# Removing sixteen small diagnostic loads, and the waits on them, from the end of a decode-attention kernel

## The chip, the cores and the metric

The kernel runs on one core of one Trainium2 chip. The metric is the device time of that core in microseconds. Two words: a transfer has landed when the last of the DMA engines that carry it has raised its semaphore, and a ring is the list of transfers that wait on one DMA engine for one queue.

## The reference, cut to what matters

Two attention blocks for a single query token. Block A has 32 heads with 32768 keys each. Block B has 32 query heads on 8 key/value heads and looks at the last 4096 keys only. Each is followed by a projection with `wo` (4096 x 512), and the two results are put side by side.

```python
def _A_ref(x, k_cache, v_cache, wq, wo):
    q = transpose((x @ wq).reshape(B, Sq, H, Dh), 0, 2, 1, 3)
    scores = einsum("bhqd,bhkd->bhqk", q, k_cache) * (Dh ** -0.5)
    o = einsum("bhqk,bhkd->bhqd", softmax(scores), v_cache)
    return transpose(o, 0, 2, 1, 3).reshape(B, Sq, H * Dh) @ wo
# _B_ref: the same with k and v cut to the last 4096 keys and repeated 4 times
return concatenate([a, b], axis=-1)          # (1, 1, 1024)
```

The caches of A alone are 2 x 32 x 8 MiB. Every byte is read once and used for one query, so this is a kernel of loads.

## The kernel before

SyncE issues nearly all loads on one queue, in program order, with its own waits for free buffers ahead of them. The part that the change touches stands at the end of the plan:

```python
for g in range(NQH):                     # 32 heads of A
    self.load_k(g, ...); self.load_v(g)  # 8 MiB each
    ...                                  # transposes, scores, softmax, P x V
self.loop = {}
for n in ("B", "A"):                     # the projections' weights, 4 MiB each
    for part in range(len(self.WO_CUTS[n]) - 1):
        self.load_wo(n, part)            # B in 2 pieces, A in 5
for i in range(16):                      # the sixteen diagnostic loads, "marks"
    self.load(self.marks[0:i + 1, 16 * i:16 * i + 16], self.X["A"]["wo"][0:i + 1, 0:16], self.marksem[i])
self.emit_spread("A")
self.emit_proj()                         # projections, store of B's half, store of A's half
for i in range(16):
    self.op("sp", lambda e, i=i: e.wait_ge(self.marksem[i], 16))
for n in ("B", "A"):
    self.op("sp", lambda e, n=n: e.wait_ge(self.outsem[n], 16))
```

Load `i` brings `i + 1` rows of 32 B into a buffer that nobody reads. B's half of the result is stored as one row (issued near 1313 us), A's half as two rows of 512 B from partitions 0 and 64; that is the last store:

```python
self.op("sp", lambda e: e.dma_start(self.out[0, :, off:off + 512].rearrange("a (i x) -> (a i) x", i=2),
                                    self.out_sb[0:65:64, :]).then_inc(self.outsem[name], 16), o)
```

Of the kernel before, what the change touches and what calls it, by code (L numbers as in the profile page):

```python
# [3 lines left out]
BF16 = mybir.dt.bfloat16  # L4
# [49 lines left out]
class _Kernel:  # L54
# [118 lines left out]
    def emit(self, eng):  # L173
# [22 lines left out]
        def body(e):  # L196
# [17 lines left out]
            for k, it in enumerate(need):  # L214
                cur, plan = {}, []
                for n in it:
                    w = []
                    for name, (sem, val) in n.items():
                        if name not in sems:
                            continue  # L220
                        rel = val - start[name] - step[name] * k
                        if rel > cur.get(name, 0):
                            cur[name] = rel
                            w.append((name, rel))
                    plan.append(sorted(w))
                plans.append(plan)
            for k, plan in enumerate(plans):
                for p, q in zip(plan, plans[-1]):
                    assert p == q or (k == 0 and set(p) <= set(q)), (eng, k, p, q)
# [37 lines left out]
    def alloc(self):  # L267
        nc = self.nc
        sb = nc.alloc_sbuf_tensor
        self.kbuf = sb("kbuf", [128, 3 * HALF * DH], BF16, align_bytes=4096)  # L270
        self.vbuf = sb("vbuf", [128, 2 * HALF * DH], BF16, align_bytes=4096)
        self.kt = [sb(f"kt{i}", [128, 1024], BF16) for i in range(NKT)]
        self.psb = sb("psb", [128, 512], BF16)
        self.ptsb = sb("ptsb", [128, 512], BF16)
        self.ident = sb("ident", [128, 128], BF16)
        self.ones = sb("ones", [128, 128], BF16)
        self.e32 = sb("e32", [128, 32], F32)
        self.spread = sb("spread", [32, 4 * 129], BF16)
        self.tr = {k: sb(f"tr_{k}", [128, 32], F32) for k in ("in", "a")}
        self.rows64 = sb("rows64", [128, 64], F32)  # L280
        self.nscale = sb("nscale", [1, 128], F32)
        self.m4 = sb("m4", [1, 128], F32)
        self.pb = sb("pb", [128, 512], F32)
        self.out_sb = sb("out_sb", [128, 256], BF16)
        self.marks = sb("marks", [16, 17 * 16], BF16)
        self.c = {}
        for name, d in self.X.items():
            HG = d["HG"]
            self.c[name] = dict(
                x=sb(f"x_{name}", [128, 12], BF16),  # L290
                oc=[sb(f"oc_{name}{i}", [128, DH + 1], F32) for i in range(2 if name == "B" else 1)],
                b=sb(f"b_{name}", [128, 32], F32),
                cm=sb(f"cm_{name}", [128, 32], F32),
                mr=sb(f"mr_{name}", [1, HG], F32),
                nb=sb(f"nb_{name}", [128, 2], F32),
                hot=sb(f"hot_{name}", [128, d["nb"]], F32),
                lh=sb(f"lh_{name}", [128, HG], F32),
                hsel=sb(f"hsel_{name}", [128, 64], F32),
                rinv=sb(f"rinv_{name}", [32, 1], F32),
                ob=sb(f"ob_{name}", [32, DH], BF16),  # L300
                oz=sb(f"oz_{name}", [128, 32], BF16),
            )

        self.qz = sb("qz", [128, 32 * self.X["B"]["NKVH"] + 64], BF16)
        self.qa = sb("qa", [128, NQH], BF16)
        self.qrow = sb("qrow", [128, 512], BF16)
        self.qw = sb("qw", [128, 64], BF16)
        self.hw = sb("hw", [128, 32], F32)
        ps = nc.alloc_psum_tensor
        self.S = ps("psS", [128, 512], F32)  # L310
        self.T = [ps(f"psT{i}", [128, 512], F32) for i in range(NT)]
        self.PT = ps("psPT", [128, 512], F32)
        self.ACC = ps("psACC", [128, 512], F32)
        self.G = ps("psG", [128, 512], F32)
        s = nc.alloc_semaphore
        self.ksem = [s(f"ksem{i}") for i in range(2)]
        self.vsem = [s(f"vsem{i}") for i in range(2)]
        self.xsem = {n: s(f"xsem_{n}") for n in self.X}
        self.wosem = {n: [s(f"wosem_{n}{i}") for i in range(len(self.WO_CUTS[n]) - 1)] for n in self.X}
        self.outsem = {n: s(f"outsem_{n}") for n in self.X}  # L320
        self.marksem = [s(f"marksem{i}") for i in range(16)]



# [69 lines left out]
    def plan(self):  # L394
        self.lsem = {"k": self.ksem, "v": self.vsem}
        self.fill = {w: [0, 0] for w in "kv"}
        self.free = {"k": [None] * 3, "v": [None] * 2}
        self.nbatch = 0
        self.copies = []
        self.pending = []  # L400
        self.psread = self.ptread = self.sread = self.accread = None
        self.gath = self.qcopy = self.hcopy = self.qread = None
        self.constants()
        a, b = self.X["A"], self.X["B"]

        self.load_wq("B")
        self.load_b("k", 0)
        self.load_wq("A")
        self.load_b("k", 1)
        self.emit_qproj("B")  # L410
        self.emit_unit("B", 0)
        self.emit_qproj("A")
        self.emit_stats("B", 0)
        self.emit_unit("B", 1, {1: lambda: self.emit_PT("B", 0)})
        self.emit_stats("B", 1)
        for g in range(2):
            if g == 1:
                self.emit_PT("B", g)
            self.load_b("v", g)
            self.emit_PV("B", g)  # L420
        self.emit_spread("B")

        for g in range(NQH):
            self.loop = {"pe": g, "dve": g // 2}
            self.load_k(g, 1 if 0 < g < NQH - 1 else 2)
            self.load_v(g)
            self.emit_qcopy(g)
            self.emit_unit("A", g)
            self.emit_stats("A", g)
            self.emit_PT("A", g)  # L430
            self.emit_PV("A", g)
        self.loop = {}
        for n in ("B", "A"):
            for part in range(len(self.WO_CUTS[n]) - 1):
                self.load_wo(n, part)
        for i in range(16):
            self.load(self.marks[0:i + 1, 16 * i:16 * i + 16], self.X["A"]["wo"][0:i + 1, 0:16], self.marksem[i])
        self.emit_spread("A")
        self.emit_proj()
        for i in range(16):  # L440
            self.op("sp", lambda e, i=i: e.wait_ge(self.marksem[i], 16))
        for n in ("B", "A"):
            self.op("sp", lambda e, n=n: e.wait_ge(self.outsem[n], 16))

# [335 lines left out]
```

## Time and profile before

| | before |
|---|---|
| time, median of 6 runs | 1324.16 us |
| span of the profiled run | 1322.0 us |
| bytes, mean rate | 570.6 MB, 432 GB/s |
| last piece of A_wo landed | 1318.87 us |
| last store issued / landed | 1319.90 / 1321.49 us |
| the sixteen loads: issued, landed | 1286.99 to 1308.00, last at 1320.64 us |

From the page of the kernel before, the DMA share in 40 slices (9 is 90% or more), the rate in the same slices, and the packet counts in all and of SyncE's queue:

```profile
DMA  9999999999999999999999999999999999999998
GB/s 404 434 435 435 436 432 436 434 436 434 431 436 436 428 438 434 430 438 432 434 436 432 434 434 434 436 432 434 437 430 436 436 430 436 434 432 436 432 434 359
DMA packets 13489, 570.60 MB, mean 432 GB/s; under 512 B 1827, under 2 KB 1830, under 8 KB 2214
...
q1 hardware_dynamic: 13190, 570.44, 99.8%
```

The engines that move the data are full until the last slice, which holds the end. A kernel like this ends when its bytes are in, plus whatever has to follow the last of them. The chain that ended last, in order of time (start, duration, what), shows how short that is:

```profile
1286.51 32.36 DMA kbuf<-in_A_wo_dram
1318.87 0.04 issue
1318.92 0.51 PE psPT L724 x6
1319.43 0.02 issue
1319.45 0.42 DVE out_sb L729
```

The last piece of A_wo is issued at 1286.51 and lands 32.36 us later, since all that was queued before it has to move first; six matmuls and one cast follow. The timeline of SyncE's issues in the same stretch (start, duration, what):

```profile
1284.72 2.23 SPq L326 DMA_DIRECT2D kbuf<-in_A_wo_dram  x5
1286.99 21.01 SPq L326 DMA_DIRECT2D marks<-in_A_wo_dram  x16
1313.40 0.24 SPq L744 DMA_DIRECT2D out_dram<-qrow  x1
1319.90 0.59 SPq L730 DMA_DIRECT2D out_dram<-out_sb  x1
```

The sixteen small loads keep SyncE for 21.01 us. SPq and ACTq are the instruction queues of SyncE and ScalarE. SyncE's waits (for whom: us in all, times, longest) show how much of it could be on the critical path:

```profile
SPq L730 <- DVE out_sb L729: 6.2, 1, 6.2
SPq L744 <- DVE qrow L743: 5.4, 1, 5.4
SPq L443 <- DMA out_dram<-out_sb: 0.5, 1, 0.5
```

After the small loads SyncE waits another 5.4 us for B's row and 6.2 us for A's.

### The profile page before, as it was taken

The page shows a single profiled execution, that of the slowest core. Times are in us where ns is not written, and L with a number is a line of the kernel's source. Part 1 is how long each engine was busy: PE and PEld are TensorE (multiplying, and loading weights), DVE is VectorE, ACT ScalarE, POOL GpSimd, SP SyncE. Part 2 cuts the span into 40 slices and gives each one's busy share as a digit, 9 for nine tenths or more (in the row PEclk, how much of TensorE's full clock was granted, in tenths as well). Part 3 has the DMA queues.
Part 4 walks back from the last instruction along what each step waited for, and adds up shares of the span by engine and source line. Part 5 has one row for each costly group of instructions (what it writes and reads, how often), then busy time and mean ns, then how long its engine had stood idle before and what let it go on. Part 6 is the DMA issues. An engine that isn't in the chain of part 4 may idle for free. (4 is left out here: it accounts for less than half of the span.)

```text
span 1322.0 us, 28805 instructions
## 1 busy us (share of the span) xinstructions
PE 966.2 (73%) x13243; PEld 674.9 (51%) x13243; DVE 751.3 (57%) x1341; ACT 54.8 (4%) x167; POOL 2.6 (0%) x22
## 2 busy tenths in 40 slices
PE   4675668777767877677787876778787677868686
PEld 3453446555444655444465544446554444655453
DVE  3663456665545666554566655556655555666463
ACT  0000000000000000000000000000000000000000
POOL 0000000000000000000000000000000000000000
PEclk8887798888779887877988788798878878888798
DMA  9999999999999999999999999999999999999998
GB/s 404 434 435 435 436 432 436 434 436 434 431 436 436 428 438 434 430 438 432 434 436 432 434 434 434 436 432 434 437 430 436 436 430 436 434 432 436 432 434 359
DMA packets 13489, 570.60 MB, mean 432 GB/s; under 512 B 1827, under 2 KB 1830, under 8 KB 2214
## 3 DMA queue, kind: packets, MB, share of 16 engines
q1 hardware_dynamic: 13190, 570.44, 99.8%
q8 instruction: 8, 0.13, 0.0%
q10 hardware_dynamic: 288, 0.00, 0.0%
q14 instruction: 3, 0.02, 0.0%
HBM read 570.43 MB, written 0.00 MB: 432 GB/s over the span
## 5 line engine op out<-in xcount | busy, mean ns | idle before, releaser
L563 DVE COPY kt<-psT 128x1024 bf16<-128x1024 bf16 x1056 | 654.9, 684 | 237.5 <-PE psT L559 235.7
L559 PE MATMUL psT<-ident,kbuf 128*128 128x128 bf16 x8448 | 579.1, 234 | 168.5 <-DMA kbuf<-in_A_k_cache_dram 154.6
L559 PEld LDWEIGHTS psT<-ident,kbuf 128*128 128x128 bf16 x8448 | 539.3, 106 | 261.0 <-DMA kbuf<-in_A_k_cache_dram 162.7
L662 PE MATMUL psACC<-vbuf,ptsb 128*4 128x512 bf16 (+1 forms) x2112 | 185.2, 527 | 23.2 <-ACT ptsb L637 21.3
L582 PE MATMUL psS<-kt,qw 128*32 128x512 bf16 x2048 | 157.6, 384 | 15.3 <-DVE kt L563 15.3
L676 DVE TENSOR_SCALAR oc_A<-psACC,hot_A 128x128 f32<-128x128 f32 x32 | 11.2, 351 | 250.1 <-PE psG L689 250.1
L662 PEld LDWEIGHTS psACC<-vbuf,ptsb 128*4 128x4 bf16 (+1 forms) x2112 | 60.4, 110 | 138.2 <-issue 91.0
L610 ACT ACTIVATE psb<-psS,nb_A 128x512 bf16<-128x512 f32 x32 | 22.0, 687 | 1165.4 <-DVE nb_A L609 1165.4
L582 PEld LDWEIGHTS psS<-kt,qw 128*32 128x32 bf16 x2048 | 34.0, 95 | 57.9 <-DVE kt L563 31.3
L689 PE MATMUL psG<-oc_A,hw 128*32 128x128 f32 (+1 forms) x128 | 19.3, 227 | 52.3 <-DVE oc_A L678 52.3
L689 PEld LDWEIGHTS psG<-oc_A,hw 128*32 128x32 f32 x128 | 11.4, 109 | 62.4 <-DVE oc_A L678 55.1
L634 PE MATMUL psPT<-ident,psb 128*128 128x128 bf16 x136 | 18.0, 275 | 34.0 <-ACT psb L610 34.0
L678 DVE SCALAR_TENSOR_TENSOR oc_A<-psACC,hot_A,oc_A 128x128 f32<-128x128 f32 x96 | 33.7, 351 | 3.4
L599 DVE TENSOR_REDUCE tr_in<-psS 128x1 f32<-128x512 f32 x34 | 23.5, 692 | 17.1 <-PE psS L582 17.1
L634 PEld LDWEIGHTS psPT<-ident,psb 128*128 128x128 bf16 x136 | 10.2, 117 | 37.0 <-ACT psb L610 36.7
L603 PE MATMUL psACC<-rows,tr_in 128*1 128x64 f32 x64 | 8.7, 217 | 25.5 <-DVE tr_in L599 25.5
L637 ACT ACTIVATE ptsb<-psPT 128x512 bf16<-128x512 bf16 x34 | 20.3, 597 | 31.1 <-PE psPT L634 31.1
L603 PEld LDWEIGHTS psACC<-rows,tr_in 128*1 128x1 f32 x64 | 2.7, 80 | 35.1 <-DVE tr_in L599 35.1
L607 PE MATMUL psACC<-mr_A,nscale 1*128 1x1 f32 x64 | 12.1, 256 | 9.7 <-DVE mr_A L606 9.7
L607 PEld LDWEIGHTS psACC<-mr_A,nscale 1*128 1x128 f32 x64 | 9.4, 182 | 15.7 <-DVE mr_A L606 15.7
L609 DVE COPY nb_A<-psACC 128x1 f32<-128x1 f32 x32 | 5.0, 157 | 15.0 <-PE psACC L607 15.0
L501 PE MATMUL psACC<-vbuf,x_B 128*2 128x512 bf16 x32 | 3.6, 627 | 13.5 <-DMA x_B<-in_B_x_dram 13.5
(81 smaller groups left out, 75.7 us busy)
## 6 DMA issues: line engine op xcount, KB each, us to landing
kbuf<-in_A_k_cache_dram SPq DMA_DIRECT2D x4, 4096.0 KB, 22.2
kbuf<-in_B_k_cache_dram SPq DMA_DIRECT2D x2, 4096.0 KB, 31.7
vbuf<-in_B_v_cache_dram SPq DMA_DIRECT2D x2, 4096.0 KB, 24.7
vbuf<-in_B_wq_dram SPq DMA_DIRECT2D x1, 4096.0 KB, 12.5
vbuf<-in_A_wq_dram SPq DMA_DIRECT2D x1, 4096.0 KB, 32.2
kbuf<-in_B_wo_dram SPq DMA_DIRECT2D x2, 2048.0 KB, 33.3
kbuf<-in_A_wo_dram SPq DMA_DIRECT2D x1, 1408.0 KB, 27.7
kbuf<-in_A_wo_dram SPq DMA_DIRECT2D x1, 1024.0 KB, 29.7
```

The lines of the kernel that those rows point to most:

```text
L559: inst = e.transpose(T[:, 128 * k:128 * k + 128], src[:, DH * k:DH * k + DH], self.ident[:, :])
L563: self.copies.append(self.op("dve", lambda v: v.tensor_copy(KT[:, :], T[:, :]), o, to="pe"))
L582: inst = e.matmul(self.S[32 * c:32 * c + 32, :], lhsT=win, rhs=self.kt[(bb + c // 2) % NKT][:, 512 * (c % 2):512 * (c % 2) + 512], start=b ...
L599: o = dve(lambda v: v.reduce_max(tr["in"][:, 0:1], self.S[:, :], axis=AXX), self.sdone, self.k_pool, to="pe" if name == "A" else None)
L603: o = self.op("pe", lambda e: e.matmul(self.ACC[0:1, 0:64], lhsT=tr["in"][:, 0:1], rhs=self.rows64[:, :], start=True, stop=True, skip_grou ...
L607: o = self.op("pe", lambda e: e.matmul(self.ACC[:, 64:65], lhsT=self.nscale[:, :], rhs=t["mr"][0:1, :], start=True, stop=True, skip_group_ ...
L610: self.sread = self.op("act", lambda s: s.activation(out=self.psb[:, :], in_=self.S[:, :], func=ACTF.Exp, bias=t["nb"][:, k:k + 1], scale= ...
L634: inst = e.transpose(PT[:, 128 * jj:128 * jj + 128], self.psb[:, 128 * jj:128 * jj + 128], self.ident[:, :])
L637: self.ptread = self.op("act", lambda s: s.activation(out=self.ptsb[:, :], in_=PT[:, 0:512], func=ACTF.Copy), self.psread, to="pe")
L662: inst = e.matmul(acc[32 * c:32 * c + rows, 0:512], lhsT=lhsT, rhs=rhs, start=begin, stop=end, tile_position=(0, 32 * c), skip_group_check ...
L678: o = self.op("dve", lambda v, src=src, hot=hot: v.scalar_tensor_tensor(out=oc, in0=src, scalar=hot, in1=oc, op0=ALU.mult, op1=ALU.add), p ...
L689: return self.op("pe", lambda e: e.matmul(self.G[0:32, c0 + c:c0 + c2], lhsT=win, rhs=t["oc"][g % len(t["oc"])][:, c:c2], start=False, sto ...
```

## The change

The loads are for diagnosis: load `i` runs on `i + 1` of the sixteen DMA engines, and from its completion one can see when those engines come to the end of the queue. The intent of the change is to take the instrument out. The diff, whole but for file names:

```diff
-        self.marks = sb("marks", [16, 17 * 16], BF16)
...
-        self.marksem = [s(f"marksem{i}") for i in range(16)]
...
             for part in range(len(self.WO_CUTS[n]) - 1):
                 self.load_wo(n, part)
-        for i in range(16):
-            self.load(self.marks[0:i + 1, 16 * i:16 * i + 16], self.X["A"]["wo"][0:i + 1, 0:16], self.marksem[i])
         self.emit_spread("A")
         self.emit_proj()
-        for i in range(16):
-            self.op("sp", lambda e, i=i: e.wait_ge(self.marksem[i], 16))
         for n in ("B", "A"):
             self.op("sp", lambda e, n=n: e.wait_ge(self.outsem[n], 16))
```

## The prediction

> What bounds the kernel. Its loads. The page gives 570.6 MB at a mean of 432 GB/s over a span of 1322.0 us, with a DMA share of 9 tenths or more in all slices but the last. In the steady part each pair of 4 MiB loads lands about 38.63 us after the pair before, 434 GB/s; the median K load lands 27.6 us after its issue (DMA issues) though it needs only 9.7 us of the engines, so the queue never runs dry. PE (73%) and DVE (57%) have slack; SyncE's 1243 us of waits for PE only pace the queue.
>
> The end (chain of waits, timeline). The last piece of A_wo is issued at 1286.5 us and lands at 1318.87, because loads are queued ahead. Then come six projection matmuls (0.51 us), the cast to out_sb (0.42), the issue of the last store (0.59, from 1319.90), its landing at about 1321.5, and about 0.45 us of closing synchronisation. The other store is issued at 1313.40.
>
> What is removed. Sixteen loads of 1 to 16 rows of 32 B, 136 data packets of 9 ns, and their completion increments. SyncE issues them from 1286.99 to 1308.00 (21.01 us, 0.256 to 7.59 us each). That looks large, but SyncE has nothing else to do until 1313.40, so it is hidden; most of it looks like back-pressure.
>
> Do they delay the real loads? The Trainium skill (DMA: Bandwidth & Descriptors, "Queues, rings and completion order") says that each DMA engine consumes descriptors in ring order. The marks come behind all of wo. The trace agrees: their packets start only from 1316.6, and on the slowest engine, which ends wo at 1318.87, its marks land after that (to about 1320.6). wo lands over the engines with a spread of 2.0 us, as K and V do without marks. The 8 MiB of wo come at 428 GB/s against 434, but its packets are smaller (121 ns for 3 KB, 2418 ns for 64 KB: about 9 ns each beyond what their bytes need), which explains that. I expect nothing here, at most 0.1 us.
>
> Do they delay the end? (a) The marks drain on the first engines until about 1320.3; the last store, on two engines, is issued at 1319.90-1320.49, and its packets start at 1321.12. It is hardly blocked, but its issue took 592 ns where the other store took 243, perhaps because the marks' completions are still being handled: 0 to 0.35 us. (b) The sixteen waits run from 1320.55 to 1321.02, while the store is under way (landed about 1321.49). They cost nothing, but for one that seems to stand behind the last store's wait: about 0.065 us. The other store, behind the marks on one engine, lands at 1320.5; nobody waits for it.
>
> Other effects: later small buffers move by 544 B in SBUF; nothing measurable expected.
>
> Prediction: 1324.14 minus about 0.25, so 1323.9 us; 8 in 10 between 1323.2 and 1324.4. Faster by over 2%: 0.01; within 2%: 0.98; slower: 0.01.
>
> What would show it: the marks and SyncE's 21 us vanish from the timeline; the last A_wo piece still lands at 1318.8 to 1318.9; the last store's issue takes 0.25 to 0.6 us and it lands up to 0.4 us sooner.
>
> What would make it wrong: the marks slow the wo loads after all (wo lands before 1318.7); the blocked SyncE, or marks in the rings, hold back something I don't see; or the new addresses change PE or DVE enough to let the queue run dry.

## The result

| | before | after |
|---|---|---|
| time, median of 6 runs | 1324.16 us (1323.98 to 1324.72) | 1324.18 us (1324.08 to 1324.66) |
| span of the profiled run | 1322.0 us | 1322.1 us |
| last piece of A_wo landed | 1318.87 us | 1318.96 us |
| last store: issue to landing | 1319.90 to 1321.49, 1.59 us | 1319.99 to 1321.59, 1.60 us |
| landing to end of span | 0.47 us | 0.46 us |
| B's store landed | 1320.53 us | 1317.05 us |

The ratio is 1.0 (95% interval 0.9987 to 1.0013). So the times show no difference, though one below 1.7 us could hide in the interval; that the change is worth nothing is read from the traces. Here and below a ratio compares all fast runs, so it is not quite the ratio of the medians that I quote.

The same lines of the page of the kernel after:

```profile
DMA packets 13217, 570.59 MB, mean 432 GB/s; under 512 B 1555, under 2 KB 1558, under 8 KB 1942
...
q1 hardware_dynamic: 12918, 570.43, 99.7%
```

SyncE's queue has 272 packets less (13190 - 12918): 136 rows of 32 B, and 136 increments of a semaphore, one for each load and engine. The chain that ended last:

```profile
1286.50 32.47 DMA kbuf<-in_A_wo_dram
1318.96 0.04 issue
1319.01 0.51 PE psPT L718 x6
1319.52 0.02 issue
1319.54 0.42 DVE out_sb L723
```

Piece by piece it is the chain of before, 0.09 us later. That tenth was there ahead of the changed code: the last V load landed at 1299.29 us before and at 1299.40 after. SyncE's issues and its waits:

```profile
1284.69 2.24 SPq L324 DMA_DIRECT2D kbuf<-in_A_wo_dram  x5
1313.34 0.32 SPq L738 DMA_DIRECT2D out_dram<-qrow  x1
1319.99 0.59 SPq L724 DMA_DIRECT2D out_dram<-out_sb  x1
```

```profile
SPq L738 <- DVE qrow L737: 26.4, 1, 26.4
SPq L724 <- DVE out_sb L723: 6.3, 1, 6.3
SPq L437 <- DMA out_dram<-out_sb: 1.0, 1, 1.0
```

The 21.01 us of issue went straight into SyncE's wait for B's row: 5.4 + 21.0 = 26.4 us. The sixteen waits behind the last store went into the wait for that store's landing, which shows as 1.0 us where it was 0.5. And the last store's issue takes 0.59 us in both kernels.

So the useful questions are why the small loads cost nothing, how near they were to costing something, and where the 0.25 us that I had forecast went.

### The profile page after: what moved, and what is told of

Same layout as the page of the kernel before. It is cut to its first block, busy times and chain, and to the rows that moved or that the text cites. A ratio compares the mean times of both kernels' runs of the same rounds, so it can differ in the third digit from the quotient of the medians.

```text
span 1322.1 us, 28781 instructions
## 1 busy us (share of the span) xinstructions
PE 967.8 (73%) x13243; PEld 677.1 (51%) x13243; DVE 752.5 (57%) x1341; ACT 54.8 (4%) x167; POOL 2.6 (0%) x22
## 3 DMA queue, kind: packets, MB, share of 16 engines
q1 hardware_dynamic: 12918, 570.43, 99.7%
## 5 line engine op out<-in xcount | busy, mean ns | idle before, releaser
L683 PE MATMUL psG<-oc_A,hw 128*32 128x128 f32 (+1 forms) x128 | 19.3, 227 | 52.4 <-DVE oc_A L672 52.4
```

The source lines that it names most:

```text
L683: return self.op("pe", lambda e: e.matmul(self.G[0:32, c0 + c:c0 + c2], lhsT=win, rhs=t["oc"][g % len(t["oc"])][:, c:c2], start=False, sto ...
```

## The experiments

My theory: the small loads were free because of their place. They stand behind every real load on the same rings, SyncE had idle time, and their landings ended before the last store's. The rivals: (R1) they did cost a few tenths, and something in the kernel after costs the same again; (R2) they are free because they are tiny, wherever they stand. All medians of "before" below are from the same chip. The outputs are right.

### e1: the buffer and the semaphores alone

```diff
 # against the kernel before
-        for i in range(16):
-            self.load(self.marks[...], ..., self.marksem[i])
...
-        for i in range(16):
-            self.op("sp", lambda e, i=i: e.wait_ge(self.marksem[i], 16))
```

> The buffer and the sixteen semaphores stay, the loads and the waits go: it tells a shift of the later buffers by 544 B from the loads. Theory (the marks are free, nothing compensates them): time within 0.3 us of before and after, last A_wo piece lands at 1318.8 to 1319.0, last store's issue to landing 1.6 us. Rival (the loads cost some tenths, and the new addresses in the kernel without marks cost the same again): 0.2 us or more below before, with an earlier landing of A_wo or a shorter end.

Measured: 1324.27 us against 1324.27 for before (ratio 0.9997, interval 0.998 to 1.0014), A_wo at 1318.92 us, the last store from issue to landing 1.59 us. R1's shifted addresses are not seen. But this profiled run took 1324.65 us, and its span of 1322.6 us was 0.5 above the others. Its chain shows why (start, duration, what):

```profile
1309.67 3.27 PE psS L733 x32
1312.94 0.02 issue
1312.96 0.70 DVE pb L736
1313.67 0.04 issue
1313.71 1.02 PE psACC L737 x2
1314.73 2.27 PE psT L741 x11
1317.00 3.04 PE psPT L720 x43
```

Here TensorE, not A_wo, ended last. B's projection ran from 1309.60 to 1312.91, 3.3 us where the kernels before and after took 1.90. Two stretches of the same profile, then of the kernel after (stretch, length, busy times of TensorE, its weight loads, VectorE, ScalarE and GpSimd, granted TensorE clock, DMA share, GB/s):

```profile
1305.00:1310.00 5.00, 2.56 (x40) 0.98 (x33) 2.09 (x7) 0.00 (x0) 0.00 (x0) 0.84 1.00 426
1310.00:1315.00 5.00, 4.20 (x37) 1.15 (x30) 0.93 (x2) 0.00 (x0) 0.00 (x0) 0.75 0.99 417
```

```profile
1305.00:1310.00 5.00, 2.56 (x48) 1.21 (x44) 2.09 (x7) 0.00 (x0) 0.00 (x0) 1.00 0.98 420
1310.00:1315.00 5.00, 4.20 (x31) 1.10 (x25) 1.37 (x2) 0.00 (x0) 0.00 (x0) 1.00 0.99 419
```

The clock granted in the last 20 us differs from run to run (0.84 and 0.75 against 1.00 and 1.00), and where it is low here and in e9 (0.84 and 0.71), the projections finish after the last load. This is a source of scatter of about half a microsecond that does not hang on the change: it is seen without the loads here and with them in e9. That it also made the slowest runs of before (1325.54 us) is likely but not shown; those runs have no profile.

### e2 and e3: the waits moved

A kernel with the loads and without any wait on them was not run, since it would end with loads that nobody waits for; that variant stays open. Instead e2 moves the waits to ScalarE, which is idle by then, and e3 puts them ahead of the last store on SyncE.

```diff
 # e2, against the kernel before
-            self.op("sp", lambda e, i=i: e.wait_ge(self.marksem[i], 16))
+            self.op("act", lambda e, i=i: e.wait_ge(self.marksem[i], 16))
```

> The sixteen loads stay; the waits go from SyncE to ScalarE, which is idle then. Theory: the waits were hidden under the last store's landing, so the end of the span after the store's landing stays at 0.47 us (before) or loses at most 0.07 us, and the span stays within 0.2 us of 1322.0. Rival (the waits cost their 0.47 us): span 0.4 us shorter.

Measured, one look: 1324.06 us, span 1322.0 us, and 0.46 us from the last store's landing to the end. The theory holds: the waits were hidden, wholly. What I had taken for one wait too many behind the last store (0.065 us in the prediction) is not there either.

```diff
 # e3, against the kernel before
+        for i in range(16):                       # now just ahead of the last store
+            self.op("sp", lambda e, i=i: e.wait_ge(self.marksem[i], 16))
         self.store("A", self.PT, 0, o)
...
-        for i in range(16):
-            self.op("sp", lambda e, i=i: e.wait_ge(self.marksem[i], 16))
```

> The same loads and waits, but the waits stand ahead of the last store on SyncE. Theory: the marks' last landing is at 1320.64, the store is otherwise issued at 1319.90, so the store is issued at 1320.7 to 1321.1 and the kernel gets 0.8 to 1.2 us longer. Rival (marks and waits are free because they are tiny, wherever they stand): no change over 0.2 us.

Measured: 1325.07 us (1324.91 to 1325.11) against 1324.27 (1323.97 to 1325.54), 0.8 us more by the medians. The ratio's interval (0.9987 to 1.002) contains 1, because two runs of before were slow; but no run of e3 was under 1324.9, and five of the seven of before were. The timeline of SyncE has the last store where it was forecast:

```profile
1320.76 0.60 SPq L728 DMA_DIRECT2D out_dram<-out_sb  x1
```

The last of the small loads landed at 1320.61 us. But in this profile TensorE was late too: the cast ran from 1320.15 to 1320.57, so that without the waits the store would have been issued at about 1320.60, 0.03 us after the cast as in before. Of the delay in this profile the waits made only the last 0.15 us. The other three runs, all a little longer, have no profile. What the trace does show is a floor: with the waits there the store can't be issued before the last small load has landed, at 1320.61, against 1319.90 in before. That is an estimate of 0.7 us for a run in which TensorE is in time. The times fit it and speak against R2, but e3 alone doesn't settle it; e4, e6 and e10 do.

### e4: the small loads ahead of wo

```diff
 # against the kernel before
+        for i in range(16):
+            self.load(self.marks[...], ..., self.marksem[i])
         for n in ("B", "A"):
             for part in range(len(self.WO_CUTS[n]) - 1):
                 self.load_wo(n, part)
-        for i in range(16):
-            self.load(self.marks[...], ..., self.marksem[i])
```

> The sixteen loads go onto SyncE's queue ahead of all loads of wo. Theory A (order in the rings protected the real loads, and a mark holds its ring for the 0.17 to 0.2 us that lay between its landings in the trace of before): the slowest engine, with nine marks, and the first ones, with up to sixteen, lose 1.5 to 3.2 us; A_wo's last piece lands at 1320 to 1322, time 1325.3 to 1327. Theory B (a mark costs its ring only its packets, 2 x 9 ns each, so at most 0.3 us): time within 0.4 us of before, A_wo lands by 1319.3. Rival C (SyncE's 21 us of issue are a cost that was hidden): loads of wo issued some 20 us later, a gap in the queue, several us longer.

Measured: 1325.03 us (1324.99 to 1325.10) against 1324.16 (1323.93 to 1325.22): 0.87 us more by the medians, with A_wo at 1319.78. The ratio's interval contains 1 here too (0.9989 to 1.0022); six of the seven runs of before lie below all four of e4. Neither A (1320 to 1322) nor B (by 1319.3) is right: the truth lies between. SyncE's issues:

```profile
1273.15 5.73 SPq L326 DMA_DIRECT2D marks<-in_A_wo_dram  x16
1278.93 0.88 SPq L326 DMA_DIRECT2D kbuf<-in_B_wo_dram  x2
1284.79 11.62 SPq L326 DMA_DIRECT2D kbuf<-in_A_wo_dram  x5
```

Rival C falls, and the 21 us are explained: the sixteen loads now take 5.73 us to issue, and it is the five pieces of A_wo that take 11.62 us where they took 2.23. The length belongs to whoever issues next when the rings are full, not to the small load.

What a small load costs its ring can be worked out from the semaphore records of the trace: from the mean landing over the sixteen engines of the last V load to that of A_wo it is 19.58 us before and 20.41 us here. The sixteen loads put 8.5 of them on an engine on average (136 / 16), so each holds its ring for (20.41 - 19.58) / 8.5, about 0.10 us. That is less than the 0.17 to 0.20 us between their landings, and some five times the 18 ns of its two packets.

### e5: the small loads on ScalarE's queue

```diff
 # against the kernel before
-            self.load(self.marks[...], ..., self.marksem[i])
+            self.op("act", lambda e, i=i: e.dma_start(
+                self.marks[...], ...).then_inc(self.marksem[i], 16))
```

> The sixteen loads go to ScalarE's queue, whose rings are empty, issued after the last head's work at about 1300 us, in the midst of wo's loads. Theory A (a mark holds up its engine for 0.2 us wherever it runs): A_wo lands 1 to 3 us later. Theory B (only packets of 9 ns, and another ring's data goes on meanwhile): A_wo lands within 0.3 us of 1318.9, time within 0.4 us. Both: SyncE's 21 us disappear from its timeline; ScalarE's issue takes under 8 us in all if SyncE's long issues were back-pressure from full rings, some 21 us if they are the price of such a load itself.

Measured: 1324.05 us (1323.86 to 1324.27) against 1324.16, A_wo at 1318.65 us. ScalarE's issues after the last head's work:

```profile
1299.46 0.49 ACTq L437 DMA_DIRECT2D marks<-in_A_wo_dram  x1
...
1299.98 5.47 ACTq L437 DMA_DIRECT2D marks<-in_A_wo_dram  x15
```

Some 6 us of issue, as the back-pressure account has it, and theory B for the rings. The packets of the small loads moved from 1303.2 to 1314.0, in the midst of wo, on the same DMA engines. The mean from V to A_wo is 19.67 us, so a small load cost (19.67 - 19.58) / 8.5, about 0.01 us: its packets, and no more. (In the ten other kernels, which have no small loads ahead of wo, this mean lies between 19.57 and 19.58 us, so 0.09 us stands clear of the noise.) The contrast with e4 is instructive. The same 136 rows on the same engines cost ten times as much on the ring that carries the real loads. The Trainium skill (DMA: Bandwidth & Descriptors, "Issuing engines are not separate DMA queues") says that issuing from several engines saves only the sequencer's time, because all run on the same sixteen DMA engines. For large loads this has nothing to set against it. For these small ones, about 0.09 us each was saved besides. But e5 changed two things: the queue, and the spacing, since the packets came over 10.8 us among large ones where in e4 they came within 2.1 us, one behind another. Which of the two saved the time was not tested. That an engine fills the pauses of one ring with packets of another is my reading of it; no run shows the inside of an engine.

### e6: thirty-two loads

```diff
 # against the kernel before
-        for i in range(16):
-            self.load(self.marks[...], ..., self.marksem[i])
+        for r in range(2):
+            for i in range(16):
+                self.load(self.marks[... 272 * r + 16 * i ...], ..., self.marksem[i])
...
-            ... e.wait_ge(self.marksem[i], 16))
+            ... e.wait_ge(self.marksem[i], 32))
```

> Thirty-two loads instead of sixteen, at the same place, ended by waits for both. Theory (free only while they drain before the last store needs the rings and SyncE): the second sixteen land on the first two engines one every 0.17 to 0.2 us after the first, until about 1323.2, so the last store's data starts some 1.5 to 2.8 us later and the kernel gets 1.5 to 3 us longer; the store of B's half is issued later than 1313.4. Rival (the loads are too small to matter): within 0.3 us of before.

Measured: 1325.92 us (1325.83 to 1326.04) against 1324.16 (1323.93 to 1325.22), 1.76 us more, with all four runs above all seven. (Ratio 1.0012, interval 0.9995 to 1.0028.) The size was right, and B's store was issued later, at 1314.93, as expected; the way was not. The last store was issued as ever, and its data packets started at 1321.02 us, not later:

```profile
1319.80 0.59 SPq L732 DMA_DIRECT2D out_dram<-out_sb  x1
```

Only its landing was late:

| us | before | e6 |
|---|---|---|
| start of the last data packet of a small load | 1318.6 | 1318.5 |
| start of the first data packet of the last store | 1321.13 | 1321.02 |
| B's store landed | 1320.53 | 1323.25 |
| last store landed, the later of its two engines | 1321.49 | 1323.43 |

So a small load's cost here is in its completion. On one engine the increments come one after another, 0.17 to 0.2 us apart, long after the data, and a later transfer's increment stands behind them.

### e8, e9, e10: more loads of one row

This account says that what counts is the number of small loads on the last store's engines, not the sum over all engines. A load of one row runs on the first engine alone, so sixteen of them give that engine as many more as e6 did, with 16 instead of 136 completions.

```diff
 # against the kernel before; n = 4, 8, 16
         for i in range(16):
             self.load(self.marks[...], ..., self.marksem[i])
+        for j in range(n):
+            self.load(self.marks[0:1, ...], self.X["A"]["wo"][0:1, 0:16], self.marksem[0])
...                    # marks grows by 16 * n columns; marksem[0] is waited for at 16 * (n + 1)
```

> Four more loads of one row after the sixteen; all go to the first engine. Theory (landings of one engine come 0.177 us apart, in order, and the last store's landing waits for those ahead of it on its engines; before had 1321.49 - 1320.53 - 0.18, about 0.8 us, to spare): B's store lands at about 1321.2, the last store is not delayed, time within 0.2 us of before. Rival (the sum of small loads over all engines counts, as the doubling's 136 rows cost 1.8 us): 4 rows cost 0.05 us. Here both say no change.

> Eight more loads of one row. Theory: B's store lands at about 1321.95, the last store at about 1322.1, so +0.4 to +0.8 us in time; its data packets are read at 1321.1 as ever. Rival (sum over all engines): +0.1 us.

> Sixteen more loads of one row, 16 completions more where the doubling had 136. Theory (one engine's row of landings): B's store lands at about 1323.3, the last store at about 1323.5, +1.6 to +2.1 us, as much as the doubling. Rival (sum over all engines): +0.2 us.

| extra one-row loads | time, median (lowest to highest), us | B's store landed | last store landed, its two engines |
|---|---|---|---|
| none (before, same chip) | 1324.20 (1323.82 to 1325.09) | - | - |
| 4 | 1324.39 (1323.93 to 1324.73) | 1320.72 | 1321.62, 1321.63 |
| 8 | 1324.48 (1324.35 to 1325.04) | 1322.00 | 1322.47, 1322.48 |
| 16 | 1326.04 (1325.74 to 1326.09) | 1323.30 | 1321.79, 1323.48 |

The ratios are 1.0, 1.0 and 1.0012; none of their intervals excludes 1, so again what separates e10 is that all its runs lie above all of before, and the trace. With sixteen the cost is 1.84 us, as much as for the doubling with its 136, and the rival falls. The last line shows it best: one row of the last store landed at 1321.79, 1.59 us after the issue as in before, and the other, on the engine with the extra loads, 1.69 us later, though both were issued by one instruction:

```profile
1320.20 0.59 SPq L732 DMA_DIRECT2D out_dram<-out_sb  x1
```

SyncE's waits in e10 name the row of B, which stands ahead of it on that engine:

```profile
SPq L445 <- DMA out_dram<-qrow: 2.0, 1, 2.0
```

With four loads nothing is visible in the time, as both sides expected. But B's store landed at 1320.72, not at the 1321.2 forecast: the first engine landed its first small load at 1317.09, 0.53 us earlier than in before (1317.62). The order in which the engines finish differs from run to run, and the room that is left differs with it. With eight the time is 0.28 us up by the medians, under the 0.4 to 0.8 that I expected, and the profile can't decide: TensorE was late in it as in e1, so the store was issued at 1320.89 and landed 1.59 us later, undelayed, although B's store landed at 1322.00 as forecast. So the threshold is not pinned down. It lies between 4 and 16 loads and depends on how late the store is anyway.

The Trainium skill (DMA: Bandwidth & Descriptors, "Queues, rings and completion order") says that each engine's increment is a strongly ordered write that lands only after that engine's earlier writes. The landings here agree: e10's 1321.79 and 1323.48 differ by engine, and on the slower one the last store lands after B's, as they were issued. The page's rule for the number of engines ("Why a DMA increments its semaphore by 16 and not by 1": the largest number up to 16 that divides the row counts of both sides) agrees too: a load of `i + 1` rows shows `i + 1` landings for every `i` from 0 to 15.

### e7: the last store in two

My prediction read the 592 ns of the last store's issue as a delay by the small loads. The kernel after has the same 592 ns, so that is false. What is it, then?

```diff
 # against the kernel after
-        self.op("sp", lambda e: e.dma_start(<both rows>, self.out_sb[0:65:64, :]).then_inc(...), o)
+        for i, q in enumerate(("sp", "act")):
+            self.op(q, lambda e, i=i: e.dma_start(<row i>, self.out_sb[64 * i:64 * i + 1, :]).then_inc(...), o)
+        self.op("dve", lambda v: v.tensor_copy(self.m4[0:1, 0:1], self.m4[0:1, 1:2]))   # carries the second signal
...                                                            # A's outsem is waited for at 32
```

> The kernel without marks, with the last store of two 512 B rows split in two stores of one row, one issued by SyncE and one by ScalarE (a small copy on VectorE between them carries the second signal). If the 592 ns of the last store's issue come from its two rows on two engines, each one-row store is issued in 0.24 to 0.33 us, as B's was, and the end from out_sb to the close gets 0.1 to 0.3 us shorter. If 592 ns are the price of a store at that moment, each takes 0.55 us or more and nothing is gained.

The end of the timeline (start, duration, engine, what):

```profile
1319.58 0.42 DVE L723 CAST out_sb<-psPT 65x256 bf16<-65x256 f32 x1 [3.69 <-PE psPT L718]
1319.92 0.13 DVE L727 COPY m<-m 1x1 f32<-1x1 f32 x1
1320.04 0.51 ACTq L725 DMA_DIRECT2D out_dram<-out_sb  x1
1320.08 0.25 SPq L725 DMA_DIRECT2D out_dram<-out_sb  x1
```

SyncE's one-row store is issued in 0.25 us, at the same moment of the kernel, so the 592 ns belong to the form of the two-row store and not to the moment. Two rows alone don't explain them: the small load of two rows was issued in 236 ns in e4 and in 249 ns in e5. What in that store takes the time (its direction, its rows 64 partitions apart) stays open. ScalarE's store takes 0.51; the first of its loads in e5 took 0.49 and the fifteen after it 0.25 to 0.41, so in both kernels the first issue on that queue after compute was a long one. Both landed by 1321.33, 1.33 us after the cast's end at 1320.00; in the kernel after this took 1.62 us (1319.96 to 1321.59). The gain of 0.30 us is real in the trace and lost in the times: 1324.15 us (1323.84 to 1324.80) against 1324.16 for before. It is the one version that should beat both kernels, by 0.02%.

## Why the prediction was right or wrong

The forecast of 1323.9 us with "within 2%" at 0.98 held: 1324.18 us lies in the range of 1323.2 to 1324.4. The range was wide enough to hold no gain at all, so the number says little for the 0.25 us, which did not come. Point by point:

- "The queue never runs dry", and the time is the bytes plus a short end: right. The rate is 432 GB/s in both, and the chain of after is that of before. One figure in it is off: the loads of the steady part are 8 MiB each, not 4 (two of them in 38.63 us are the 434 GB/s), so a K load needs 19.3 us of the engines, not 9.7. That is still less than the 27.6 us to its landing, and the conclusion stands.
- SyncE's 21.01 us are hidden, "most of it looks like back-pressure": right. They reappear as 21.0 us more of waiting, and the same sixteen loads issue in some 6 us where the rings have room (e4, e5).
- The small loads do not delay wo, because they come behind it: right, and now shown rather than argued. Ahead of wo they cost 0.87 us (e4). From the last V landing to A_wo's it was 19.59 us before and 19.56 after.
- (b) The waits cost nothing: right (e2). The 0.065 us for one of them behind the store's wait was wrong: landing to end is 0.468 us before and 0.464 after.
- (a) "Its issue took 592 ns ..., perhaps because the marks' completions are still being handled: 0 to 0.35 us": this is the step that failed. The term measures zero: 592 ns in both kernels. The issue of a one-row store took 0.25 us on SyncE beside it (e7), so the length goes with that two-row store. Comparing it with B's one-row store, I had taken a difference between two transfers for a delay. These two terms are the whole 0.25 us that did not come.
- What I didn't see: the small loads came near the critical path at another point, the landings. In before, B's store landed behind them at 1320.53 us, and the last store's increment, on the same engine, at 1321.49. That left under a microsecond; sixteen more used it up and cost 1.84 us (e10).

## What to carry to other kernels

A long issue time of a queue is a cost only if the queue has something to do next, and here it came from full rings, not from the transfer that shows it: look at what the issuing engine waits for afterwards. Small transfers at the end of a queue are free while their landings end before the last store's; count them by engine, since each of them delays a later landing on its engine by almost 0.2 us. If they must stand among large loads, try them on another queue and spread out (0.01 us each here, against 0.10 in a block on the same one).

## What the Trainium skill lacked or had wrong

- DMA: Bandwidth & Descriptors, "Anatomy of one DMA — SWDGE (gpsimd) path": it calls the semaphore write "essentially free", though its table gives about 100 ns for the update. Both are said of another issue path. On the SyncE queue here, increments of small loads on one engine land 0.17 to 0.20 us apart though each packet takes 9 ns, and sixteen of them in front of a store delayed it by 1.69 us (e10).
- The same page, "Issuing engines are not separate DMA queues": only the issue time is said to be saved by a second queue. Small loads cost their engine about 0.10 us each in a block on the ring of the large loads (e4) and about 0.01 us on another queue, where they were also spread out (e5).
- The same page, "Queues, rings and completion order": consumption in ring order agrees (the small loads' packets start at 1316.6 us behind wo). It doesn't say that an issue blocks when the rings are full; one 64-byte load blocked SyncE for 7.59 us before, one piece of A_wo for 9.57 us in e4.
- No page that I read has the price of the issue of this two-row store (592 ns, against 243 to 323 ns for a store of one row on SyncE and 236 ns for a load of two rows in e4), or of the first issue on ScalarE's queue after compute (490 and 508 ns).
- No page that I read gives a figure for how far apart the engines finish one load: the first and the last of the sixteen landings of A_wo's last piece lie 1.6 to 2.6 us apart in the kernels here (2.0 in before), and the last of them is what a consumer waits for.
